# Attention and gated MLP on one core: early silu steps from exponential and reciprocal, one scale of maxima per pair, constants made on the chip, and a new order

## The chip, the cores and the metric

One core of one Trainium2 chip runs the whole program. The time is that of one execution on the device in microseconds; of several executions the median is given. The profile is a hardware trace of one execution. Its engines are PE (matrix multiply, with its weight loads as PEld), DVE (vector), ACT (scalar and activation), POOL (GpSimd) and SP, whose queue issues every DMA of this kernel.

## The reference

Two stages. An attention over 4 batches and 8 heads, 768 positions, head size 64: each query sees the keys less than 16 positions away and, besides, 24 pooled keys (the maximum over each block of 32 keys) with pooled values (the mean over the block).

```python
k_sum = k.reshape(B, H, nb, block, D).max(axis=3)
v_sum = v.reshape(B, H, nb, block, D).mean(axis=3)
scores_l = scale * (q @ k.T)            # kept where |i - j| < 16
scores_s = scale * (q @ k_sum.T) + np.log(block)
a = softmax(concatenate([masked scores_l, scores_s]))
out = a @ concatenate([v, v_sum])
```

Then a gated MLP over the 3072 tokens, d_model 512, d_ff 1536:

```python
g = x @ w_gate
silu = g * (1.0 / (1.0 + np.exp(-g)))
y = (silu * (x @ w_val)) @ w_out
```

The MLP weights arrive as 64-bit floats and are turned into 32-bit floats on the chip.

## The kernel before, in words

**Tiling.** Two heads make a pair `u` (0 to 3), a batch is cut into two halves of 384 tokens, and `k` counts the halves of all batches (0 to 7). A unit `(k,u)` of attention is: scores `SC` on PE (L575), row maxima on DVE, exponentials on ACT, sums and a reciprocal, the scaling `nrm`, two transposes `PP` on PE with copies `pt` back (L701), and the product with the values `XO` (L724). For batch 0 (`k` 0 and 1) the mask and the log of the block size are added on PE, by a matmul of an identity `id_r` with the table `parts_sb` (L602 to L615); the softmax there takes `max0` and `max1` (one per head of the pair, L650), scales each with its own small step `scl0`, `scl1` (L656, L673), and then issues three exponentials per head straight from the score bank (L663). For later batches a fused step does the mask and the minimum (L625).

**Weights.** `w_first(j)` (L961) loads 1 MB of a 64-bit weight tile, for each of the 12 slices `j` of d_ff, and decodes it: `abs` on ACT, then `clamp`, `shift`, `sign` and `low` on DVE (L920), then a split into a high part (ACT) and a low part `lo` (DVE or POOL, L954). `o_first(j)` does the same for the output weights. Later batches use sums of the weight blocks (`weight_sums`, L984); for the first two slices the sums are put off: the tile is written to DRAM as `whole` and read back as `m_again` (`deferred_sums`, L979).

**MLP, batch 0.** `u_plain(j,hf)` (L1043) makes the two products g and v for slice `j` and half `hf`. In `finish` (L1073) ACT takes the silu of g out of the bank into `a`, DVE multiplies `a` by v (`mul`), and `hidden` (L1028) splits it into `hh` and `hl`, which the output matmuls `downs` (L1203) read. Batches 1 to 3 use seven products instead of eight (`u_seven`, L1112).

**Constants.** The table of masks and logs `raw_parts`, the identity `id_sb`, and `mean_sb`, the matrix that pools the values of batch 0 in `first_means` (L762), come by DMA from arrays that the host fills; `parts_sb` and `id_r` are casts of the first two. A score bias `bias_sb` for the later batches is loaded too.

**What sets the order.** Every step is entered in a plan with the engines that may do it and a cost for each. `order` (L295) and `run` (L330) place the steps in a modelled time line: each step gets a latest start, an engine takes the ready step that is due first, and a step that two engines can do goes to the one on which it would end first, after `BIAS` has been added (POOL 0.3, the others 0). `NUDGES` (L219) then moves the due time of named steps, pins some to an engine (`d`, `a`, `p`), and gives PE steps a slack. The result is the fixed order of instructions on each engine and of the DMAs on SP's queue. Where the model sees PE idle early on, small matmuls on zeros (`warm_up`, L1215) are put in front of the next PE step; N_WARM of them open the program.

**Activation tables.** Exponential and silu need different tables on ACT; the profile shows an ACT_TABLE_LOAD ahead of the first step of the other kind.

Of the kernel before, what the change touches and what calls it, by code (L numbers as in the profile page):

```python
# [13 lines left out]
AF = mybir.ActivationFunctionType  # L14
# [7 lines left out]
P = 128  # L22
# [15 lines left out]
GROUP = 3  # L38
DEFER = 2
AGAIN = 5  # L40
# [22 lines left out]
def bias_parts() -> np.ndarray:  # L63

    m = np.zeros((P, 3 * KC + 2 * NB), np.float32)
    first = m[:, : 3 * KC].reshape(P, 3, KC)
    first[:] = score_bias()
    x = np.float32(math.log(BLK) / SCALE)
    for to in (first[:, :, KW:], m[:, 3 * KC : 3 * KC + NB], m[:, 3 * KC + NB :]):
        part = (x.view(np.uint32) & np.uint32(0xFFFF0000)).view(np.float32)  # L70
        to[:] = part
        x = np.float32(x - part)
    return m


def value_pool() -> np.ndarray:

    m = np.zeros((P, NV, NB), np.float32)
    for i in range(WIN, WIN + S):
        m[i % P, i // P, (i - WIN) // BLK] = 1.0 / BLK  # L80
    return m
# [138 lines left out]
kt(0,1) -217.9; q(0,1) -205.2; raw_parts -367.5; id_sb -346.1; mean_sb -133.9; vn(1) -330; vr(1) -256.6  # L220
kt(0,3) -191.9; q(0,3) -127.9; kt(0,0) -97; q(0,0) -125.6; kt(0,2) -102.3; q(0,2) -159.2; bias_sb +527.7
scl0(0,1) -121.6 d; eps(0,1) -37.9 d; scl0(0,3) +606.1 d; max1(0,3) -78.6; scl1(0,3) +52.2 d; nrm(0,3) -176.1 d
fv(2) +158.7 a; scl0(0,0) +51.6 d; eps(0,0) +82.2 a; rcp(0,0) -492.6; nrm(0,0) -235.8 p; pt0(0,1) +183.4 d
pt1(0,1) -91.3 d; FV(0) s0.8; max1(0,2) -216.4; exp5(0,2) +22.8; pt1(0,3) -207.7 a; odd1(1) -6.3 d; odd2(1) -66.4 p
# [12 lines left out]
raw_o4 +49.6; abs_o4 +203.3; shift_o4 -135.6; sign_o4 -36.5; mul(4,0) +271.7; hl(0,4,0) -227.1 p; kw(2,0) +190.1
vt(1,0) +188.9; pool(1,0) +471.8; vpool(1,0) +177.6; join(2,1) +148.4 p; ttr1(2,0) +650.5; exp1(2,0) -158.7
exp2(2,0) -36.6; exp3(2,0) +112.8; nrm(2,0) -156.9 p; ttr1(2,1) +373.4; exp1(2,1) -153.2; exp2(2,1) -95.1
eps(2,1) -86.9 a; silu(4,1) -38.3; clamp_w5 +467.6; low_w5 +74.3; lo_w5 -92.2 d; sumA11_w5 +165 p  # L240
sumA12_w5 +485.6 p; silu(5,0) +131.1; hl(0,5,0) +49.9 p; PP0(2,0) s2.8; pt0(2,0) -351 d; pt1(2,0) +1.5 d
pt0(2,1) +57.2; pt1(2,1) +160.5 a; mul(5,1) +224.1; hh(0,5,1) -381.6 d; hl(0,5,1) +59.7; again_w0 -34.5
sumA21_w0 -60.8 p; part(0,1,0) +157.3; q(2,2) +242.5; join(2,3) +96.7 p; XO(2,0) s0; vw(2,2) +246; vw(2,3) +479.5
exp1(2,2) +286.6; eps(2,2) -309.4 p; rcp(2,2) +73.9; ttr0(2,3) -224.2; ttr1(2,3) -122.4; exp1(2,3) +123.8
eps(2,3) +423 a; rcp(2,3) -179.7; abs_w6 +264.2; low_w6 -37; sumA21_w6 +120.4 p; raw_o6 +291.7; lo_o6 +410.1
hl(0,6,0) +119.7 d; PP0(2,2) s0.3; vs(1,2) +53.8; pt1(2,2) -139.4; vs(1,3) +41.4; hh(0,6,1) -103.9 a
hl(0,6,1) +199.7 p; sumA12_w1 +145 d; sf1 +377.4; sign_w7 -82.7; low_w7 -588.1; sumA22_w7 +111.2 d; sumA11_w7 +188 d
hl(0,7,0) +189.5; kw(3,1) +382.5; join(3,1) +22 d; XO(2,2) s3.7; exp3(3,0) +164.5; nrm(3,0) +341.8; exp3(3,1) +184
eps(3,1) +300; hh(0,7,1) +77.4 a; hl(0,7,1) -202.1 p; clamp_w8 +88.4; sumA22_w8 -305.2 p; sumA11_w8 +68.3 d
sumA12_w8 +178.9; raw_o8 +167.1; clamp_o8 -237.8; shift_o8 +118.5; hi_o8 +250.6; lo_o8 +571.8 d; silu(8,0) +242.2  # L250
hl(0,8,0) +240 p; hl(0,8,1) -72.5 d; pt0(3,0) -78.2 d; pt0(3,1) -83.9 d; q(3,2) +318.7; join(3,2) +22.3 p
kw(3,3) +51.2; XO(3,0) s4.1; nrm(3,2) +412.4 d; shift_w9 -231.9; lo_w9 -70.4 p; sumA12_w9 -232.8 p; mul(9,0) +212.2
hl(0,9,0) -138.2 p; values(3,2) -76.3 p; clamp_w10 +82.9; shift_w10 -137.4; low_w10 +319; sumA21_w10 +300.1
sumA11_w10 -50.7 p; raw_o10 +169.9; abs_o10 +355.1; clamp_o10 -369.2; shift_o10 +77.9; sign_o10 +171.1
clamp_w11 +194.6; hl(0,11,1) -195.9 p; B21l(1,0) +249.6; B22l(1,0) +236.2 p; T3h(1,1) +143.4 d; B21h(1,1) +211.6 d
B22l(1,1) +158.2 p; sh(0) +72 a; hl(1,0,0) +153.4; kw(4,0) -304.1; vpool(2,0) +153; kw(4,1) -142.5; pool(2,1) +156.5
# [176 lines left out]
def body(ctx, tc, qP, kP, kW, vT, vW, vN, vR, wgv, wo, bias, parts, ident, mean, out):  # L433
# [89 lines left out]
    def load_const(b, src, n):  # L523
        add_dma(b.name, n, lambda: make(b), lambda: src, (), (b,))
# [965 lines left out]
```

## Time and profile before

| | |
|---|---|
| median of 3 runs | 678.46 us (678.29 to 680.05) |
| the profiled execution | 681.53 us |
| its span, first to last instruction | 679.8 us |
| PE busy | 667.9 us (98%) |
| DVE busy | 513.2 us (76%) |
| ACT busy | 340.8 us (50%) |
| POOL busy | 124.4 us (18%) |
| mean granted PE clock | 0.995 of full speed |

A row of a timeline gives start, duration, engine, line, operation, tiles written and read, the number of instructions merged, and in brackets the idle time before with what ended it. Rows of groups give the count, the total busy time, the mean duration in ns, and the idle time before. PE's busy time includes the matmuls on zeros and matmuls that run slowly, so a busy PE is not the same as a PE that gets on with its work.

### The profile page before, as it was taken

To read this page: it belongs to the slowest core of one execution; us is meant where nothing else is said; L and a number is where in the kernel's file an instruction comes from. 1 tells how busy PE (TensorE), PEld (TensorE's weight loads), DVE (VectorE), ACT (ScalarE), POOL (GpSimd) and SP (SyncE) were. 2 spreads that over 40 slices of the span, in tenths; PEclk is the share of its full clock that TensorE was granted. 3 is DMA by queue.
4 is the path that set the end of the run, shared out by engine and by line. 5 is a ranking of instruction groups with operands and counts; after the bars stand their busy time and mean duration, and the time that the engine had idled before them with its cause. 6 is when DMAs were issued, how large, how long until landed. Compare 5 with 4: busy or idle time off the path is not lost.

```text
span 679.8 us, 13325 instructions
## 1 busy us (share of the span) xinstructions
PE 667.9 (98%) x5097; PEld 616.2 (91%) x5097; DVE 513.2 (76%) x1135; ACT 340.8 (50%) x850; POOL 124.4 (18%) x115
## 2 busy tenths in 40 slices
PE   8999999999999999999999999999999999999997
PEld 8789899899899998989999898989999898989896
DVE  4899998999999786977758883766768762646464
ACT  2888757677664386644544265744535233313130
POOL 0615306504412130112413140100001000000000
PEclk8999999999999999999999999999999999999999
DMA  9999558878657588785957584663715462535232
GB/s 326 374 341 351 186 215 305 319 273 286 226 200 256 219 283 289 256 282 198 279 227 232 189 301 144 248 212 136 248 39 204 181 221 104 218 108 217 109 109 93
DMA packets 40111, 153.06 MB, mean 225 GB/s; under 512 B 4400, under 2 KB 9328, under 8 KB 33136
## 3 DMA queue, kind: packets, MB, share of 16 engines
q1 hardware_dynamic: 40048, 152.21, 63.5%
q8 instruction: 40, 0.66, 0.4%
q14 instruction: 23, 0.19, 0.1%
HBM read 116.54 MB, written 35.65 MB: 224 GB/s over the span
## 4 chain that ended last, share of the span: by engine, by line
PE 76%; DVE 11%; DMA 7%; issue 2%; ACT 2%; POOL 1%; SPq 0%; DVEq 0%; ACTq 0%; POOLq 0%
PE p L1105 37%; PE acc L1177 25%; PE g L1064 4%; PE v L1064 3%; PE sc L598 3%; PE xo L747 2%; PE pp L714 2%; DVE m_w L949 1%; DVE m_w L943 1%; DMA s<-ss 1%; DMA kw<-in_kW 1%; DMA s<-sf 1%; DVE w L489 1%; DMA raw_w<-in_wgv 1%; DVE m_w L930 1%
## 5 line engine op out<-in xcount | busy, mean ns | idle before, releaser
L1177 PE MATMUL acc<-o,hh 128*128 128x512 f32 x570 | 177.3, 392 | 0.0
L1177 PEld LDWEIGHTS acc<-o,hh 128*128 128x128 f32 x570 | 105.7, 188 | 21.9 <-issue 1.0
L1105 PE MATMUL p<-xh_T,s 128*128 128x384 f32 x432 | 122.6, 339 | 0.9 <-DVE s L489 0.4
L1177 PE MATMUL acc<-o,hl 128*128 128x512 f32 x285 | 111.4, 391 | 0.0
L1105 PE MATMUL p<-xh_B,wa 128*128 128x384 f32 x288 | 84.8, 335 | 0.0
L1105 PEld LDWEIGHTS p<-xh_T,s 128*128 128x128 f32 x432 | 79.0, 188 | 3.1 <-DMA s<-ss 1.1
L484 ACT COPY s<-p 128x384 f32<-128x384 f32 x61 | 29.2, 479 | 90.5 <-PE p L1105 83.3
L1105 PE MATMUL p<-xl_T,s 128*128 128x384 f32 x216 | 72.3, 335 | 0.0
L489 DVE TENSOR_TENSOR part<-acc,part 128x512 f32<-128x512 f32 x71 | 47.5, 685 | 29.0 <-PE acc L1177 29.0
L1177 PEld LDWEIGHTS acc<-o,hl 128*128 128x128 f32 x285 | 53.5, 188 | 11.6 <-DVE hl L489 0.3
L641 ACT ACTIVATE p<-p,nm 128x120 f32<-128x120 f32 x144 | 55.2, 385 | 11.7 <-DVE nm L629 10.2
L489 DVE TENSOR_TENSOR c<-p,u 128x384 f32<-128x384 f32 x72 | 39.6, 552 | 20.2 <-PE p L1105 20.2
L1064 PE MATMUL g<-xh_B,w 128*128 128x384 f32 x192 | 54.1, 340 | 0.4 <-DVE w L489 0.3
L1064 PE MATMUL v<-xh_B,w 128*128 128x384 f32 x192 | 53.2, 335 | 0.0
L1105 PEld LDWEIGHTS p<-xh_B,wa 128*128 128x128 f32 x288 | 53.0, 188 | 0.1
L484 ACT CAST hh<-a 128x384 fp32r<-128x384 f32 x47 | 24.1, 514 | 51.5 <-DVE a L489 47.6
L489 DVE TENSOR_TENSOR hl<-a,hh 128x384 fp32r<-128x384 f32 x77 | 45.9, 596 | 3.6 <-ACT hh L484 0.4
L1105 PE MATMUL p<-xl_B,wa 128*128 128x384 f32 x144 | 48.1, 334 | 0.0
L489 DVE TENSOR_TENSOR a<-c,a 128x384 f32<-128x384 f32 x65 | 40.7, 626 | 5.1 <-ACT a L1040 2.5
L1105 PE MATMUL p<-xh_B,s 128*128 128x384 f32 x144 | 42.4, 334 | 0.0
L1105 PE MATMUL p<-xh_T,wa 128*128 128x384 f32 x144 | 42.3, 334 | 0.0
L1105 PEld LDWEIGHTS p<-xl_T,s 128*128 128x128 f32 x216 | 40.6, 188 | 0.3
(151 smaller groups left out, 1353.8 us busy)
## 6 DMA issues: line engine op xcount, KB each, us to landing
wa<-wa SPq DMA_DIRECT2D x36, 768.0 KB, 4.3
s<-ss SPq DMA_DIRECT2D x24, 1024.0 KB, 7.2
raw_w<-in_wgv SPq DMA_DIRECT2D x12, 1024.0 KB, 6.6
ss<-s SPq DMA_DIRECT2D x12, 1024.0 KB, 7.6
wa<-w SPq DMA_DIRECT2D x12, 768.0 KB, 5.5
kw<-in_kW SPq DMA_DIRECT2D x24, 360.0 KB, 5.6
vw<-in_vW SPq DMA_DIRECT2D x28, 288.0 KB, 4.9
kt<-in_kP SPq DMA_DIRECT2D x16, 400.0 KB, 5.5
```

The costliest lines, as they stand in the source:

```text
L484: nc.scalar.copy(out, in_)
L489: vector[e].tensor_tensor(out=out, in0=a, in1=b, op=op)
L598: nc.tensor.matmul(make(sc[h])[s * QT : (s + 1) * QT, c * KC + at : c * KC + at + x.shape[-1]], make(q)[hs, qs], x, start=not biased or c ...
L641: nc.scalar.activation(out=make(p)[:, i, :], in_=make(p)[:, i, :], func=AF.Exp, scale=-1.0, bias=make(nm)[:, i : i + 1], accum_out=make(sm ...
L714: nc.tensor.transpose(make(pp)[:KC, c * P : (c + 1) * P], make(p)[:, g * NT // 2 + c, :], make(id_sb))
L747: nc.tensor.matmul(ps[hs, qs], v, make(pt)[:, h, qs], start=True, stop=True)
L930: lambda e: nc.vector.tensor_scalar(out=make(m), in0=make(m), scalar1=F64_LO, scalar2=F64_HI, op0=ALU.max, op1=ALU.min), (), (m,),
L943: lambda e: nc.vector.scalar_tensor_tensor(out=bits(), in0=high(), scalar=-0x40000000, in1=bits(), op0=ALU.bitwise_and, op1=ALU.bitwise_or ...
L949: lambda e: nc.vector.scalar_tensor_tensor(out=bits(), in0=low(), scalar=29, in1=bits(), op0=ALU.logical_shift_right, op1=ALU.bitwise_or), ...
L1064: nc.tensor.matmul(t[:, :TOK], a, x, start=u == order_of[0] and i == 0, stop=u == order_of[-1] and i == 2,)
L1105: nc.tensor.matmul(t[:, :TOK], a, x, start=first and kk == 0 and n == 0, stop=kk == 1 and n == 2, skip_group_check=not first,)
L1177: nc.tensor.matmul(ps[:, :wide], a, w, start=j == js[0] and m == 0, stop=j == js[-1] and m == 2)
```

## The change

Seven things are changed.

1. **Silu from the exponential.** For the first half (`hf == 0`) of slices 0 to 3, silu is made as g / (1 + exp(-g)): ACT takes exp(-g) out of the bank into `a`; `more` adds one (DVE or ACT); `inv` takes the reciprocal on DVE; `gate` multiplies by g from the bank on DVE. `mul` and the rest follow as before.
2. **One scale.** `scl` scales the six maxima of a pair in one step after both maxima.
3. **Constants on the chip.** `raw_parts`, `id_sb` and `mean_sb` are filled by memsets (DVE or POOL) and by affine selects on POOL; three DMAs and three input arrays go.
4. **Put-off sums.** AGAIN goes from 5 to 10, so `deferred_sums` for slices 0 and 1 stand after slices 10 and 11.
5. **Reserve behind DMAs.** In the model a DMA that ends between 60 and 215 us counts as 2.5 us later for steps of DVE, ACT and POOL.
6. **Bias.** BIAS of DVE goes from 0 to 0.5, and `join` may also be put on ACT.
7. **Nudges.** The whole table NUDGES is replaced by another, so the order on each engine and of the DMAs comes out anew.

```diff
+BY_EXP = 4
+ONE_SCALE = True
-AGAIN = 5
+AGAIN = 10
...
+SAFE, SAFE_FROM, SAFE_TO = 2.5, 60.0, 215.0
-BIAS = {DVE: 0.0, ACT: 0.0, POOL: 0.3}
+BIAS = {DVE: 0.5, ACT: 0.0, POOL: 0.3}
...
+vn(1) -212.9; kt(0,3) +7.8; q(0,3) +11.6; kt(0,0) +11.9; q(0,0) +9; kt(0,2) +8.9; q(0,2) +11.6; vn(0) +11.4
...
+        more = SAFE if s.engine == DMA and SAFE_FROM < s.end < SAFE_TO else 0.0
-            at[o] = max(at[o], (s.end + lag) if o.after[s] else s.start)
+            at[o] = max(at[o], s.end + lag + more * (not {PE, DMA} & set(o.engines)) if o.after[s] else s.start)
...
+    def make_constants():
+        masks = lambda: make(raw_parts)[:, : 3 * KC].rearrange("p (v c) -> p v c", c=KC)
+        add_fill("id one", id_sb, None, P, lambda: make(id_sb), 1.0)
+        add_choose("id here", id_sb, None, P, lambda: make(id_sb), [[-1, P]], 0, ALU.is_equal, 0.0)
+        logs = log_parts()
...
+            add_fill(f"log{x}", raw_parts, f"l{x}", NB, to, logs[x])
+        add_fill("mask none", raw_parts, "m", 3 * KW, lambda: masks()[:, :, :KW], 0.0)
+        for s in range(2):
...
+            add_choose(f"mask{s} above", raw_parts, "m", 3 * KW, to, [[0, 3], [-1, KW]], 2 * WIN - 1, ALU.is_ge, MASK)
+            add_choose(f"mask{s} below", raw_parts, "m", 3 * KW, to, [[0, 3], [1, KW]], -1, ALU.is_ge, MASK, rows=-1)
+        add_fill("mask first", raw_parts, "m", WIN, lambda: masks()[:QT, 0, :WIN], MASK)
+        add_fill("mask last", raw_parts, "m", WIN, lambda: masks()[QT:, 2, WIN + QT : KW], MASK)
+        add_fill("mean all", mean_sb, None, NV * NB, lambda: make(mean_sb), 1.0 / BLK)
+        add_choose("mean above", mean_sb, None, NV * NB, lambda: make(mean_sb), [[P, NV], [-BLK, NB]], -WIN, ALU.is_ge, 0.0)
+        add_choose("mean below", mean_sb, None, NV * NB, lambda: make(mean_sb), [[-P, NV], [BLK, NB]], WIN + BLK - 1, ALU.is_ge, 0.0, rows=-1)
...
-            f"join({k},{u})", (POOL, DVE), NT * NB, lambda: make(kw)[:, :, KW:],
+            f"join({k},{u})", (POOL, DVE, ACT), NT * NB, lambda: make(kw)[:, :, KW:],
...
-                plan.add(f"scl{g}({k},{u})", {DVE: 0.14, ACT: 0.18}, lambda e, g=g: shrink(e, g), (), ((nm, g),))
...
+                elif g == 1:
+                    plan.add(f"scl({k},{u})", {DVE: 0.14, ACT: 0.18}, lambda e: shrink(e, None), (), (nm,))
...
+    def silu_by_exp(name, a, src, reads):
+        plan.add(
+            f"{name}", {ACT: 0.49},
+            lambda e: nc.scalar.activation(out=make(a), in_=src(), func=AF.Exp, scale=-1.0), reads, (a,), table="exp",
+        )
...
+        plan.add(f"more{name[4:]}", {DVE: cost(DVE, "scalar", TOK), ACT: cost(ACT, "copy", TOK)}, one_more, (), (a,))
+        plan.add(f"inv{name[4:]}", {DVE: 0.53}, lambda e: nc.vector.reciprocal(out=make(a), in_=make(a)), (), (a,), port=False)
+        add_tt(f"gate{name[4:]}", (DVE,), TOK, lambda: make(a), src, lambda: make(a), ALU.mult, reads, (a,))
...
-            silu(f"silu({j},{hf})", a, lambda: make(ps["g"])[:, :TOK], (ps["g"],))
+            by = silu_by_exp if hf == 0 and j < BY_EXP else silu
+            by(f"silu({j},{hf})", a, lambda: make(ps["g"])[:, :TOK], (ps["g"],))
```

More of the change, by code (lines that the diff above doesn't have):

```diff
@@ L60, in score_bias, with log_parts @@
     return m
[L63 to L67, printed above, removed]
+def log_parts() -> list:
+    out = []
     x = np.float32(math.log(BLK) / SCALE)
-    for to in (first[:, :, KW:], m[:, 3 * KC : 3 * KC + NB], m[:, 3 * KC + NB :]):
+    for _ in range(3):
         part = (x.view(np.uint32) & np.uint32(0xFFFF0000)).view(np.float32)
-        to[:] = part
+        out.append(float(part))
         x = np.float32(x - part)
[L73 to L81, printed above, removed]
+    return out
 PE, DVE, ACT, POOL, DMA = "PE", "d", "a", "p", "q"
@@ L219 @@
 NUDGES = """
[L220 to L224, printed above, removed]
@@ L240 @@
[L240 to L244, printed above, removed]
@@ new lines @@
+part(0,1,5) +78; abs_w6 +29.7; sumA12_w6 -6.1 d; wa6 +113.8; hl(0,6,0) +26.2 p; PP1(2,3) s2.3; hh(0,6,1) -38.8 d
+abs_w7 -169.2; sign_w7 +84.5; low_w7 +84.5; hi_w7 -51; sumA21_w7 +52 p; hl(0,7,0) -8.3 d; q(3,0) +133.3
+join(3,0) +51.4 a; join(3,1) +43.9 a; XO(2,3) s1.3; exp0(3,1) +65.6; rcp(3,1) +112.4; nrm(3,1) +12.1 d
+clamp_w8 +91.8; lo_w8 -91.5 p; sumA12_w8 +1.4 d; sf8 +59.7; clamp_o8 +224.2; shift_o8 +37.1; sign_o8 -25.3
+lo_o8 +109.8 d; silu(8,0) +124.7; hl(0,8,0) -79.4 p; hh(0,8,1) -36.3 d; PP0(3,0) s7.9; pt0(3,0) -83.2 d
@@ L432, in body @@
 @with_exitstack
-def body(ctx, tc, qP, kP, kW, vT, vW, vN, vR, wgv, wo, bias, parts, ident, mean, out):
+def body(ctx, tc, qP, kP, kW, vT, vW, vN, vR, wgv, wo, bias, out):
     nc = tc.nc
@@ L521, in body, with add_fill, add_choose @@
     mean_sb = buf("pro", "mean", [P, NV, NB], "mean_sb")
+    def add_fill(name, b, part, cols, to, value):
+        plan.add(
+            name, {DVE: 0.1 + 0.0006 * cols, POOL: 0.1 + 0.0012 * cols},
+            lambda e: vector[e].memset(to(), value), (), ((b, part),),
+        )
+    def add_choose(name, b, part, cols, to, pattern, base, keep, other, rows=1):
+        plan.add(
+            name, {POOL: 0.1 + 0.0012 * cols},
+            lambda e: nc.gpsimd.affine_select(
+                out=to(), in_=to(), pattern=pattern, compare_op=keep, fill=other, base=base, channel_multiplier=rows,
+            ), (), ((b, part),),
+        )
+    def make_constants():
[3 more added lines that the diff above has]
+        logs = log_parts()
+        for x, to in enumerate((lambda: masks()[:, :, KW:], lambda: make(raw_parts)[:, 3 * KC : 3 * KC + NB], lambda: make(raw_parts)[:, 3 * KC + NB :])):
+            add_fill(f"log{x}", raw_parts, f"l{x}", NB, to, logs[x])
+        add_fill("mask none", raw_parts, "m", 3 * KW, lambda: masks()[:, :, :KW], 0.0)
+        for s in range(2):
+            rows = slice(s * QT, (s + 1) * QT)
+            to = lambda rows=rows: masks()[rows, :, :KW]
+            add_choose(f"mask{s} above", raw_parts, "m", 3 * KW, to, [[0, 3], [-1, KW]], 2 * WIN - 1, ALU.is_ge, MASK)
[5 more added lines that the diff above has]
+        add_choose("mean below", mean_sb, None, NV * NB, lambda: make(mean_sb), [[-P, NV], [BLK, NB]], WIN + BLK - 1, ALU.is_ge, 0.0, rows=-1)
     def load_const(b, src, n):
@@ L672, in a_softmax @@
                 plan.add(f"max{g}({k},{u})", {DVE: 0.50}, lambda e, g=g: greatest(g), (sc[g],), ((nm, g),))
-                plan.add(f"scl{g}({k},{u})", {DVE: 0.14, ACT: 0.18}, lambda e, g=g: shrink(e, g), (), ((nm, g),))
+                if not ONE_SCALE:
+                    plan.add(f"scl{g}({k},{u})", {DVE: 0.14, ACT: 0.18}, lambda e, g=g: shrink(e, g), (), ((nm, g),))
+                elif g == 1:
+                    plan.add(f"scl({k},{u})", {DVE: 0.14, ACT: 0.18}, lambda e: shrink(e, None), (), (nm,))
             else:
@@ L1036, in hidden, with one_more @@
         )
+    def silu_by_exp(name, a, src, reads):
+        plan.add(
+            f"{name}", {ACT: 0.49},
+            lambda e: nc.scalar.activation(out=make(a), in_=src(), func=AF.Exp, scale=-1.0), reads, (a,), table="exp",
+        )
+        def one_more(e):
+            if e == ACT:
+                nc.scalar.activation(out=make(a), in_=make(a), func=AF.Copy, bias=1.0)
+            else:
+                vector[e].tensor_scalar(out=make(a), in0=make(a), scalar1=1.0, scalar2=None, op0=ALU.add)
+        plan.add(f"more{name[4:]}", {DVE: cost(DVE, "scalar", TOK), ACT: cost(ACT, "copy", TOK)}, one_more, (), (a,))
+        plan.add(f"inv{name[4:]}", {DVE: 0.53}, lambda e: nc.vector.reciprocal(out=make(a), in_=make(a)), (), (a,), port=False)
+        add_tt(f"gate{name[4:]}", (DVE,), TOK, lambda: make(a), src, lambda: make(a), ALU.mult, reads, (a,))
     def silu(name, a, src, reads):
@@ L1313, in body @@
         if u == 1:
[L1314 to L1315 removed]
+            make_constants()
             add_copy("parts", (POOL, ACT, DVE), 3 * KC + 2 * NB, lambda: make(parts_sb), lambda: make(raw_parts), (raw_parts,), (parts_sb,))
             add_copy("idr", (POOL, ACT, DVE), P, lambda: make(id_r), lambda: make(id_sb), (id_sb,), (id_r,))
[L1318 removed]
             load_first_values(1)
```

88 lines of the change are left out of this document (36 added, 52 removed).

## The prediction

> **What bounds the kernel now.** I read the busy time by stage first, then PE's groups and what they wait for, then the timelines of the first 60 us.
>
> ```profile
> core 0: us, PE busy (x) PEld busy (x) DVE busy (x) ACT busy (x) POOL busy (x), PEclk, DMA share, GB/s
> 10.00:20.00 10.00, 10.00 (x172) 8.55 (x163) 6.37 (x15) 3.77 (x21) 0.99 (x2) 0.66 1.03 411
> 20.00:60.00 40.00, 37.36 (x524) 34.19 (x524) 39.69 (x62) 34.48 (x96) 18.24 (x18) 1.00 0.96 358
> 60.00:220.00 160.00, 158.33 (x1275) 144.94 (x1273) 153.22 (x326) 107.27 (x249) 53.98 (x44) 1.00 0.73 255
> 220.00:670.00 450.00, 449.08 (x3037) 416.55 (x3036) 309.71 (x726) 193.45 (x485) 51.04 (x49) 1.00 0.57 199
> ```
> ```profile
> L1218 PE MATMUL pp<-warm 128*128 128x128 f32 x22 | 3.0, 284 | 0.7 <-DVE xl_B L489 0.7
> ...
> L1218 PE MATMUL xo<-warm 128*128 128x128 f32 x16 | 2.2, 281 | 0.7 <-ACT p L665 0.7
> ```
>
> From 220 us on PE is busy 449.08 of 450 us: it sets the pace there, and no edit takes a matmul of the MLP away. From 60 to 220 us only 1.67 us are free. From 20 to 60 us PE is idle for 40 - 37.36 = 2.64 us, and 3.0 + 2.2 = 5.2 us of its busy time are matmuls on zeros, put where the plan expected PE to wait: 7.8 us in which PE gets nowhere. DVE is busy 39.69 of these 40 us, ACT 34.48, POOL only 18.24. So this stage belongs to DVE, with ACT close behind. The other open time is the start, before the first scores. I sum the edits against the profiled execution, 681.53 us; the median of the runs, 678.46, lies 3.07 us below it.
>
> **Constants on the chip.** SP's queue at the start, the landing of the query that PE waits for, how full the DMA engines are, and the sizes:
>
> ```profile
> 0.72 0.39 SPq L503 DMA_DIRECT2D raw_parts<-in_parts  x1
> 1.16 0.42 SPq L503 DMA_DIRECT2D id_sb<-in_ident  x1
> ...
> 3.04 0.43 SPq L503 DMA_DIRECT2D q<-in_qP  x1
> ```
> ```profile
> 3.04 5.80 DMA q<-in_qP
> ```
> ```profile
> 6.00:8.00 2.00, 1.64 (x15) 1.45 (x14) 0.54 (x1) 0.51 (x1) 0.00 (x0) 1.00 1.03 382
> ```
> ```profile
> raw_parts<-in_parts SPq DMA_DIRECT2D x1, 204.0 KB, 2.5
> ...
> id_sb<-in_ident SPq DMA_DIRECT2D x1, 64.0 KB, 2.2
> ```
>
> The query lands at 8.84 us, with the DMA engines full (1.03). Ahead of it go 268 KB that fall away: at 382 GB/s 0.7 us. By issues it is more: the new nudges put `vn(1)` first and leave key and query to their own due times, so the query could be third, at 0.72 + 2 x 0.44 = 1.6 us, 1.4 us earlier. I take 0.9 us, nearer to the bytes, as the engines are full. The third load, `mean_sb`, stands behind the query.
>
> What takes the place of the DMAs is POOL work: one identity select, four mask selects of 288 columns and two of 168, besides fills that DVE can share. No select is in this trace. The nearest rows are a copy with one input and a step with two:
>
> ```profile
> L486 POOL COPY kw<-ks 128x144 f32<-128x144 f32 x11 | 6.2, 568 | 40.4 <-PE p L1105 24.4 <-DMA kw<-in_kW 8.9 <-issue 4.1
> ```
> ```profile
> L489 POOL TENSOR_TENSOR m_w<-m_w 128x256 f32<-128x256 f32 x18 | 21.4, 1197 | 35.5 <-ACT w L484 24.2 <-DVE w L489 7.7 <-DVE m_w L489 2.6
> ```
>
> The five selects for identity and mask take 2.9 us at 0.57 each, 6.0 us at 1.2 each, from about 0.8 us on. The table is wanted when the first scores run, near 8.0 us after the edit, with two casts ahead of it. I take no cost: at the dearer row POOL ends near 7 us. If a select costs 2 us, the first scores come some 3 us late. Term: -0.9.
>
> **One scale.**
>
> ```profile
> L661 DVE TENSOR_SCALAR nm<-nm 128x3 f32<-128x3 f32 x8 | 1.6, 214 | 0.0
> ```
>
> Sixteen small scales, eight of them on DVE as this row shows, become eight: about 0.8 us of DVE, half of it in the stage that it binds, so -0.4 in DVE's sum below. The added wait: the exponentials of the first head wait for the second maximum as well, and behind them on ACT wait the rest of that unit and the copies `pt`. Where both maxima stand side by side on DVE this is nothing; elsewhere it is what DVE puts between them, and the plan can give ACT other work. I take 0, up to 0.5 us.
>
> **Silu from the exponential.** What ACT does around the first silu, PE beside it, and the loads that bring the exponential back:
>
> ```profile
> 45.47 1.28 ACT L1040 ACT_TABLE_LOAD   x1
> 46.77 0.49 ACT L1040 ACTIVATE a<-g 128x384 f32<-128x384 f32 x1
> 47.15 0.20 ACT L659 ACTIVATE nm<-nm 128x3 f32<-128x3 f32 x1
> 47.37 1.28 ACT L665 ACT_TABLE_LOAD   x1
> ...
> 50.36 0.88 ACT L484 COPY pt<-pp 120x384 f32<-120x384 f32 x2
> ```
> ```profile
> 48.92 0.87 PE L714 MATMUL pp<-id_sb,p 128*120 128x128 f32 x6
> 50.54 1.60 PE L1218 MATMUL xo<-warm 128*128 128x128 f32 x12 [0.75 <-ACT p L665]
> ```
> ```profile
> L665 ACT ACT_TABLE_LOAD x3 | 3.8, 1283 | 0.1
> ```
>
> Three loads bring the exponential back, and each has one to silu before it: six loads, 7.7 us of ACT, of which all but one to silu fall away. The first two, 2.57 us, stand ahead of the copies `pt` at 50.36. PE's transposes end at 49.79 and the product starts at 52.1: 2.3 us lost. Without the loads the two copies can follow the transposes at once, 0.9 us, and PE loses 0.9 to 1.0: I take -1.4 (0 if DVE delivers the scores later, -1.7 if DVE takes one copy). The loads after 60 us meet a PE with 1.67 us to win: -0.5. The Trainium skill, ScalarE: Activation LUTs, section What ACT_TABLE_LOAD costs, adds about 1.38 us of drain to each load; here the next ACTIVATE starts 0.02 us after the load ends (45.47 + 1.28, then 46.77), so the trace disagrees; by the page the six loads would be worth 16 us of ACT, an estimate, not 7.7.
>
> DVE pays for it. The rows for `more`, `gate` and `inv`, and last the copies and casts that DVE does from 20 to 60 us (its column is the first):
>
> ```profile
> L486 DVE CAST hh<-a 128x384 fp32r<-128x384 f32 x49 | 18.6, 379 | 0.9
> ...
> L489 DVE TENSOR_TENSOR a<-v,a 128x384 f32<-128x384 f32 x24 | 13.1, 547 | 0.0
> ```
> ```profile
> L690 DVE RECIPROCAL ri<-sm x32: 147/180/192, 19.2 to 495.1; 128x6 f32<-128x6 f32 x32
> L687 DVE TENSOR_SCALAR sm<-sm x8: 160/170/174, 19.0 to 461.8; 128x6 f32<-128x6 f32 x8
> ```
> ```profile
> 20.00:60.00 40.00, 2.53 (x6) 8.71 (x11) 1.00 0.96 358
> ```
>
> `more` is 0.38, `gate` 0.55. For `inv` the trace has reciprocals of 6 columns only. Beside the scalar step of the same 6 columns their median is 10 ns longer and their shortest 13 ns shorter, so the nearest row shows no price per column. Low end: 0.55, as `gate`. Middle: the 10 ns as a price of 6 columns, 64 x 10 ns = 0.64 more, 1.2 us. (A far higher end is the last rival.) I take 0.55. A step is then 1.48 us, and three of the four fall before 60 us: +4.4. Against it stand the scales, -0.4, and the copies: with 0.5 of bias against DVE and an ACT that is 7.7 us lighter, most of the 2.53 us can go to ACT: -2.2. POOL has 21.8 us free there, and I expect one low part or one scaling of a unit to pass to it: -1.5. DVE's sum: +0.3, from -1 (more passes) to +3 (`inv` at 1.2, less passes).
>
> **Reserve, put-off sums, bias of `join`.**
>
> ```profile
> DVE kw L486 <- DMA kw<-in_kW: 7.8, 6, 2.2
> ```
> ```profile
> 200.00:220.00 20.00, 20.00 (x146) 18.59 (x145) 19.83 (x41) 10.55 (x21) 3.96 (x2) 1.00 0.69 240
> ```
> ```profile
> L489 POOL TENSOR_TENSOR m_again<-m_again 128x256 f32<-128x256 f32 x4 | 4.2, 1055 | 6.2 <-DMA m_again<-whole 3.1 <-DVE m_again L489 2.9
> ```
>
> DVE stands 7.8 us behind late loads of `kw`, with all its later steps queued behind that `join`. A reserve, or `join` on ACT, puts other work first. But PE has 1.67 us to win, 0.5 of it counted: -0.7, from 0 to -1.2. Moving the sums takes their two loads and two stores on SP, and four POOL steps of 1.06 us, away from slices 5 and 6 and adds them near 200 us, where POOL is busy 3.96 of 20 us but DVE 19.83. I cost that at nothing because POOL covers it; if DVE gets them, the late one is the first store of sums, which the seven products need from about 226 us: 1 to 2 us. After 220 us PE has 0.92 us free, so a new order wins next to nothing there and can lose: 0, up to +2.
>
> **The sum.** -0.9 - 1.4 - 0.5 + 0.3 - 0.7 = -3.2: 678.3 us as a profiled execution, 675.3 beside the median. All terms at their best: -1.4 - 1.7 - 0.5 - 1.0 - 1.2 = -5.8, 672.7. At their worst: -0.7 + 3 + 2 = +4.3, 682.8. About 0.3% (2 us) is what a measurement of this kernel can tell from no change.
>
> **The rivals.**
>
> *The clock stays up (more gain).*
>
> ```profile
> 13.00:18.00 5.00, 5.00 (x48) 3.92 (x40) 2.77 (x6) 1.36 (x8) 0.00 (x0) 0.50 1.03 415
> ```
>
> From 13 to 18 us PE is granted half its clock, and nobody else is full (DVE 2.77, ACT 1.36 of 5 us). If earlier first scores escape that, these 5 us of matmuls shrink toward 2.5; I count 2 of it: 673.3. For it: the query comes earlier. Against: the same small matmuls follow in the same order of units.
>
> *Nothing is won (the same).* DVE's stage does not move: what ACT is spared waits behind DVE anyway, and three steps of 1.48 us eat what copies and scales give. Then the start remains, less up to 1 us: 677.6 to 678.5.
>
> *The reciprocal is long (slower).* From the copies of DVE a fixed part can be read: 379 ns for 384 columns above and
>
> ```profile
> L486 DVE COPY kw<-ks 128x144 f32<-128x144 f32 x13 | 2.9, 225 | 7.8 <-DMA kw<-in_kW 7.8
> ```
>
> give 0.64 ns a column and 133 ns fixed. If the reciprocal has that fixed part, its 180 ns leave 47 ns for 6 columns, 7.8 ns each, and 384 of them take 3.1 us. Three such steps hold DVE 3 x 2.55 = 7.7 us longer where it is full; less the 3.2 us that the rest gives, +4.5: 683. It decides against the change from `inv` = 0.55 + 3.2/3 = 1.6 us. Against it: the scalar step of 6 columns, nearer in shape, has no smaller a time. The Trainium skill, VectorE: DVE Perf Modes, section First, the fixed hardware budget, calls the reciprocal an iterative divide with a repeat count of 8, which speaks for this rival; the trace has no wide one and leaves it open.
>
> **How the numbers follow.** Forecast 0.46, clock stays up 0.13, nothing won 0.20, long reciprocal 0.16, late mask or late sums 0.05 (about 681). Faster 0.59, same 0.20, slower 0.21. The forecast's own range is 672.7 to 677; the whole one runs from 669.5, the clock's rival with the best terms, to 681.5, and leaves out most of the long reciprocal.
>
> **What would show it.** Right: no table load between the first exponentials and the first true silu, scores from about 8 us, fewer zeros ahead of `xo` near 50 us, `inv` at 0.55 us, DVE full from 20 to 60 us. Wrong: `inv` over 1.6 us, selects on POOL past 8 us, or PE waiting after 220 us.

## The result and the profile after

The kernel with the change takes 689.27 us (median of 4 runs, 686.51 to 690.79), the kernel before in the same comparison 678.38 us (678.22 to 680.05): a ratio of 1.015, 95% interval 1.0114 to 1.0187. It is slower by 10.9 us, where 3.2 us less was forecast. The profiled execution took 688.82 us with a span of 687.1 us. PE is busy 668.0 us in it, against 667.9 before, so of the 7.3 us by which this span is longer all but 0.1 are idle time of PE. (The profiled execution of before lies 3.07 us above its median, so the medians stand further apart than the spans.) Where that time lies, stage by stage, after:

```profile
core 0: us, PE busy (x) PEld busy (x) DVE busy (x) ACT busy (x) POOL busy (x), PEclk, DMA share, GB/s
20.00:60.00 40.00, 34.95 (x485) 32.11 (x481) 39.84 (x56) 29.99 (x84) 13.86 (x13) 0.96 1.00 369
60.00:90.00 30.00, 25.78 (x239) 21.92 (x238) 27.79 (x40) 17.12 (x47) 6.42 (x5) 1.00 0.46 151
90.00:220.00 130.00, 130.00 (x1028) 120.61 (x1027) 124.47 (x254) 88.51 (x207) 51.22 (x49) 1.00 0.77 271
220.00:440.00 220.00, 219.57 (x1574) 202.05 (x1572) 155.77 (x362) 127.34 (x308) 65.26 (x54) 1.00 0.67 235
440.00:470.00 30.00, 27.34 (x259) 23.55 (x254) 18.55 (x72) 18.54 (x62) 1.38 (x5) 0.94 0.62 206
```

And the two later stages of before:

```profile
60.00:90.00 30.00, 29.06 (x264) 26.45 (x262) 28.05 (x44) 21.15 (x50) 10.86 (x8) 1.00 0.72 250
440.00:470.00 30.00, 30.00 (x239) 27.27 (x238) 19.90 (x60) 14.24 (x42) 0.00 (x0) 1.00 0.47 163
```

PE loses 37.36 - 34.95 = 2.4 us from 20 to 60 us, 3.3 us from 60 to 90, and 2.7 us from 440 to 470, a stretch for which the prediction had only "0, up to +2". DVE is still full from 20 to 60 us (39.84 of 40), while ACT fell from 34.48 to 29.99 and POOL from 18.24 to 13.86: what ACT was spared did not become time of PE. The wide reciprocal, which no trace of before held, beside the narrow one:

```profile
L1067 DVE RECIPROCAL a<-a 128x384 f32<-128x384 f32 x4 | 10.2, 2546 | 0.0
L706 DVE RECIPROCAL ri<-sm 128x6 f32<-128x6 f32 x32 | 5.6, 180 | 10.3 <-POOL sm L703 5.9 <-ACT sm L701 4.0
```

One `inv` takes 2.55 us, not 0.55, and 378 more columns cost 2546 - 180 = 2366 ns, 6.26 ns each. PE's largest waits:

```profile
PE acc L1210 <- DVE a L469: 3.3, 2, 2.4
PE acc L1210 <- ACT hh L464: 2.7, 1, 2.7
PE pp L730 <- DVE p L709: 2.6, 2, 2.2
```

The first and third lie in the stages with reciprocals, the second is the one near 450 us. In the timeline of PE the two that come out of the early stages are these, the idle time in brackets:

```profile
48.18 1.51 PE L730 MATMUL pp<-id_sb,p 128*120 128x128 f32 x6 [2.17 <-DVE p L709]
...
66.00 0.73 PE L1210 MATMUL acc<-o,hh 128*128 128x512 f32 x2 [2.44 <-DVE a L469]
```

How the reciprocal gets there is seen on DVE ahead of the first one. After:

```profile
42.26 2.55 DVE L1067 RECIPROCAL a<-a 128x384 f32<-128x384 f32 x1
44.72 0.47 DVE L664 TENSOR_REDUCE nm<-sc 128x3 f32<-128x360 f32 x1
45.10 0.54 DVE L469 TENSOR_TENSOR a<-g,a 128x384 f32<-128x384 f32 x1
45.56 0.52 DVE L664 TENSOR_REDUCE nm<-sc 128x3 f32<-128x360 f32 x1
46.00 0.18 DVE L706 RECIPROCAL ri<-sm 128x6 f32<-128x6 f32 x1
46.10 0.52 DVE L469 TENSOR_TENSOR a<-v,a 128x384 f32<-128x384 f32 x1
...
47.13 0.90 DVE L709 TENSOR_TENSOR p<-p,ri 128x720 f32<-128x720 f32 x1
```

There is no bracket: DVE never stops. `nrm` (L709) stands in the queue behind `inv` though it needs nothing from it, and ends at 48.03; the transposes on PE wait for it and start at 48.18. A gap of PE can also cost what follows it. The clock granted to PE (the third column from the end) in the two stretches after this gap, after the one of 2.44 us that ends at 66 us, and after the one near 450 us that is told next:

```profile
48.00:50.00 2.00, 1.82 (x8) 1.85 (x9) 2.00 (x3) 1.74 (x7) 0.60 (x1) 0.50 1.00 412
50.00:52.00 2.00, 2.00 (x10) 2.00 (x9) 2.00 (x4) 1.28 (x4) 0.00 (x0) 0.65 1.01 413
...
66.00:68.00 2.00, 2.00 (x20) 1.46 (x22) 2.00 (x4) 0.51 (x1) 0.61 (x1) 1.00 0.00 0
...
454.00:456.00 2.00, 2.00 (x8) 1.43 (x8) 1.52 (x3) 0.23 (x1) 0.00 (x0) 0.54 0.05 20
```

After two of the three gaps the clock fell, after the one at 66 us it did not.

The loss near 450 us has another cause. POOL, then DVE behind it, then PE:

```profile
446.68 0.30 POOL L466 COPY kw<-ks 128x144 f32<-128x144 f32 x1 [7.34 <-PE p L1138]
447.07 0.23 POOL L703 TENSOR_SCALAR sm<-sm 128x6 f32<-128x6 f32 x1
450.96 0.30 POOL L466 COPY kw<-ks 128x144 f32<-128x144 f32 x1 [3.66 <-DMA kw<-in_kW]
451.35 0.23 POOL L703 TENSOR_SCALAR sm<-sm 128x6 f32<-128x6 f32 x1
```
```profile
451.62 0.19 DVE L706 RECIPROCAL ri<-sm 128x6 f32<-128x6 f32 x1 [2.95 <-POOL sm L703]
```
```profile
453.81 0.93 PE L1210 MATMUL acc<-o,hh 128*128 128x512 f32 x2 [2.66 <-ACT hh L464]
```

These are `join(7,0)`, the small step `eps(6,2)` on the sums of unit (6,2), `join(7,1)` and `eps(6,3)`. `join(7,1)` waits 3.66 us for a late load of `kw`, and `eps(6,3)`, which needs no load, stands behind it on POOL. DVE waits 2.95 us for that step, the casts `hh` on ACT come late, and PE waits 2.66 us. So two suspects come out of the trace: the price of `inv`, and the place of one `join`.

### The profile page after: what moved, and what is told of

Same layout as the page of the kernel before. It is cut to its first block, busy times and chain, and to the rows that moved or that the text cites. A ratio compares the mean times of both kernels' runs of the same rounds, so it can differ in the third digit from the quotient of the medians.

```text
span 687.1 us, 13339 instructions
## 1 busy us (share of the span) xinstructions
PE 668.0 (97%) x5083; PEld 614.8 (89%) x5083; DVE 501.9 (73%) x1043; ACT 366.6 (53%) x912; POOL 160.6 (23%) x164
## 4 chain that ended last, share of the span: by engine, by line
PE 80%; DVE 9%; DMA 7%; ACT 1%; issue 1%; POOL 1%; SPq 0%; DVEq 0%; ACTq 0%; POOLq 0%
PE p L1138 34%; PE acc L1210 27%; PE g L1096 6%; PE v L1096 6%; PE xo L763 3%; PE sc L611 2%; PE pp L730 2%; DMA s<-ss 2%; DVE a L1067 1%; DMA raw_w<-in_wgv 1%; DMA kw<-in_kW 1%; DMA s<-sf 1%; DMA whole<-m_w 1%; DMA q<-in_qP 1%; DVE p L709 1%
## 5 line engine op out<-in xcount | busy, mean ns | idle before, releaser
L464 ACT CAST hh<-a 128x384 fp32r<-128x384 f32 x78 | 40.0, 513 | 77.6 <-DVE a L469 76.8
L464 ACT COPY s<-p 128x384 f32<-128x384 f32 x65 | 31.2, 479 | 69.2 <-PE p L1138 68.7
L469 DVE TENSOR_TENSOR hl<-a,hh 128x384 fp32r<-128x384 f32 x75 | 44.9, 599 | 16.6 <-ACT hh L464 13.8
L469 DVE TENSOR_TENSOR a<-c,a 128x384 f32<-128x384 f32 x62 | 38.9, 628 | 6.1 <-ACT a L1072 3.7
L469 DVE TENSOR_TENSOR u<-p,s 128x384 f32<-128x384 f32 x36 | 19.9, 553 | 32.1 <-ACT s L464 30.6
```

What stands on the lines that cost most here:

```text
L464: nc.scalar.copy(out, in_)
L469: vector[e].tensor_tensor(out=out, in0=a, in1=b, op=op)
```

## The experiments

Each ran in turn with the kernel before on one chip, in three batches (experiments 1, 2, 3 and 5; then 7; then 4, 6 and 8), the third on another chip than the first two; the median of the kernel before was 679.86, 679.01 and 678.92 us. So batches are compared by their ratios to it, and a gain in us is a ratio times 679 us. Unless it is said otherwise, the order of the steps on each engine is that of the kernel named, so that nothing but the edit differs.

**1. The reciprocal made short (theory: price of `inv`; rival: the new order itself is bad).** In the kernel after, `inv` keeps its place but is a multiplication. Here, in 3 and for half of the steps in 4, the kernel leaves out the reciprocal, so its values are not those of silu:

```diff
-        plan.add(f"inv{name[4:]}", {DVE: 0.53}, lambda e: nc.vector.reciprocal(out=make(a), in_=make(a)), (), (a,), port=False)
+        plan.add(f"inv{name[4:]}", {DVE: 0.53}, lambda e: tt(e, make(a), make(a), make(a), ALU.mult), (), (a,), port=False)
```

> The changed kernel with every instruction in its place, only that `inv` multiplies `a` by itself instead of taking the reciprocal, so the gate's value is not silu. Theory 1, the wide reciprocal (2.55 us in the trace, four of them) starves PE between 40 and 85 us: `inv` falls to about 0.55 us, DVE is relieved of 8 us, PE's waits on DVE at 48, 66 and 73 us shrink, and the time falls by 4 to 6 us, to 683 to 685. Rival, the new order and not the reciprocal is what costs: the waits move to the next late step of DVE and the time stays at 687 or above. The wait near 451 us stays in either case.

Measured: 680.0 us, ratio 1.0011 (0.9989 to 1.0032). Against the 1.015 of the kernel after that is 0.0139, about 9.4 us, for four steps that are 4 x 2.0 = 8.0 us shorter on DVE. The price of the reciprocal is thus most of the loss. That the loss is more than the length of the steps is not shown: the intervals of the two ratios leave about 3 us either way.

**2. The join moved (theory: the late load blocks POOL; rival: the loss near 450 us follows from the early one).** In the kernel after, one step changes its place on POOL:

```diff
-    for s in order(plan.steps):
+    line = order(plan.steps)
+    late = next(s for s in line if s.name == "join(7,1)")
+    line.remove(late)
+    line.insert(1 + next(i for i, s in enumerate(line) if s.name == "eps(6,3)"), late)
+    for s in line:
```

> The changed kernel with one step moved: on POOL, join(7,1) goes behind eps(6,3) instead of ahead of it. Theory 2, one small POOL step stood behind a join that waits for a late load, and through it DVE, ACT and PE stood still near 451 us: the wait of PE on `hh` (2.7 us) and the half clock after it go, and the time falls by 4 to 4.5 us, to about 685. Rival, something else is late there as soon as this is gone (the scaling, the table load): less than 2 us. Rival 2, the stall is there in only some executions, since the spread of the changed kernel is 4 us: the fastest runs stay at 686.5 and only the slow ones come down.

Measured: 686.76 us, ratio 1.0103 (1.0075 to 1.0130): 0.0047 less, about 3.2 us. The stage, of the kernel with the join moved:

```profile
440.00:470.00 30.00, 30.00 (x318) 26.57 (x317) 21.20 (x77) 21.79 (x71) 3.38 (x8) 1.00 0.70 230
```

PE is busy throughout; from 20 to 90 us it is not, with 34.53 of 40 and 25.76 of 30 us, as in the kernel after. In experiment 1 the stall near 450 us was still there (27.82 of 30 us). So each loss is there without the other. The intervals of 1.015 and 1.0103 overlap, and the fastest runs of the two kernels, 686.51 and 686.35 us, are alike, which the second rival (a stall in some executions only) would give as well. Against it stands the same move made on the kernel of experiment 1, in one batch (experiment 3): the median falls from 680.0 to 677.4 us and the fastest run from 678.33 to 675.68. The move is worth 2.6 to 3.7 us.

**3. Both.** Edits 1 and 2 together.

> Both edits: the short `inv` (not silu's value) and join(7,1) behind eps(6,3). If the two causes are independent, the gains add, 8 to 10.5 us, and the time is 679 to 681, within 3 us of the kernel before. If the order as such costs something more, it stays above 682.

Measured: 677.4 us, ratio 0.9956 (0.9933 to 0.9979). The gains add up: 0.0139 + 0.0047 = 0.0186 against the 0.0194 from 1.015 to 0.9956. With both causes taken away no loss is left. DVE of this run, to set beside the timeline of the kernel after:

```profile
41.98 0.55 DVE L469 TENSOR_TENSOR a<-a 128x384 f32<-128x384 f32 x1
42.45 0.53 DVE L664 TENSOR_REDUCE nm<-sc 128x3 f32<-128x360 f32 x1
42.89 0.55 DVE L469 TENSOR_TENSOR a<-g,a 128x384 f32<-128x384 f32 x1
43.35 0.52 DVE L664 TENSOR_REDUCE nm<-sc 128x3 f32<-128x360 f32 x1
43.79 0.18 DVE L706 RECIPROCAL ri<-sm 128x6 f32<-128x6 f32 x1
43.89 0.52 DVE L469 TENSOR_TENSOR a<-v,a 128x384 f32<-128x384 f32 x1
...
45.23 0.90 DVE L709 TENSOR_TENSOR p<-p,ri 128x720 f32<-128x720 f32 x1
```

The same steps in the same order; from the start of `inv` to that of `nrm` it is 3.25 us instead of 4.87.

**4. Two reciprocals of four (does each cost the same, or only those before 60 us?).** As 3, but slices 0 and 1 keep the true reciprocal.

```diff
+            lambda e: nc.vector.reciprocal(out=make(a), in_=make(a)) if name in ("silu(0,0)", "silu(1,0)") else tt(e, make(a), make(a), make(a), ALU.mult),
```

> The changed kernel with join(7,1) behind eps(6,3); `inv` is the true reciprocal for slices 0 and 1 and a multiplication (not silu's value) for slices 2 and 3. None true gave 677.4, four true 686.8. If each reciprocal costs PE its 2 us of DVE wherever it stands: half way, 681.5 to 682.5. If, as the prediction had it, only those ahead of 60 us count (slices 0, 1 and the third's start): 683 to 685. If the late ones count because PE had run out of stock by then: 678.5 to 680.5.

Measured: 680.67 us, ratio 1.0028 (1.0014 to 1.0042). From 0.9956 with none to 1.0103 with four, two give 0.0072 of 0.0147, half: within the intervals the two after 60 us cost as much as the two before. The stages agree. From 20 to 60 us PE is busy 34.73 us, as with all four (34.53; 36.97 with none), and from 60 to 90 us 29.04, as with none (25.76 with all four).

**5. A silu without the reciprocal.** As 3, but silu as 0.5 g (1 + tanh(g/2)): ACT takes the tanh in place of the exponential, `more` and `inv` issue nothing, `gate` does (a + 1) g, and `mul` brings the factor 0.5. It is the same function in another form.

```diff
-            lambda e: nc.scalar.activation(out=make(a), in_=src(), func=AF.Exp, scale=-1.0), reads, (a,), table="exp",
+            lambda e: nc.scalar.activation(out=make(a), in_=src(), func=AF.Tanh, scale=0.5), reads, (a,), table="exp",
...
-        add_tt(f"gate{name[4:]}", (DVE,), TOK, lambda: make(a), src, lambda: make(a), ALU.mult, reads, (a,))
+            lambda e: nc.vector.scalar_tensor_tensor(out=make(a), in0=make(a), scalar=1.0, in1=src(), op0=ALU.add, op1=ALU.mult),
```

> The whole computation again, in the order of the changed kernel with join(7,1) behind eps(6,3): silu of the early steps as 0.5 g (1 + tanh(g/2)). ACT takes tanh in place of the exponential, `more` and `inv` emit nothing, `gate` is (a + 1) g and `mul` is 0.5 a v, so a step costs DVE 0.55 us beside `mul` instead of 3.5. If the reciprocal was the cost and the edit's idea (one table early) is sound, 1 us or more better than with both edits above: 677 to 680, and no table load between the early exponentials and the first true silu. If avoiding the loads is worth nothing, no better than that kernel.

Measured: 675.87 us, ratio 0.994 (0.992 to 0.9961), below both kernels. Its two early stages:

```profile
20.00:60.00 40.00, 36.97 (x499) 34.03 (x498) 39.34 (x59) 31.66 (x94) 17.16 (x14) 1.00 1.01 376
60.00:90.00 30.00, 29.86 (x260) 26.30 (x259) 27.77 (x42) 20.50 (x42) 5.49 (x4) 1.00 0.72 250
```

The loss of 60 to 90 us is gone (25.78 there in the kernel after).

**6. What the saved table loads are worth in the new order.** As 5, but silu comes from its own table: the six early loads are back and DVE has none of the added steps.

```diff
+            lambda e: nc.scalar.activation(out=make(a), in_=src(), func=AF.Silu), reads, (a,), table="exp",
...
+        plan.add(f"gate{name[4:]}", on((DVE,), "tt", TOK), lambda e: None, reads, (a,))
```

> The order of the changed kernel with join(7,1) behind eps(6,3), every step in its place, but the early silu steps are the true silu of ACT's table again (`more`, `inv` and `gate` emit nothing): the table loads come back and DVE has nothing to pay. Against the same kernel with tanh (675.9 us, ratio 0.994) this gives the price of the loads alone in this order. If the loads are worth what the prediction said (1.4 + 0.5 us, less DVE's `gate` of 3 x 0.55): within 1.5 us, 675.5 to 677.5. If ACT is the late engine in this order: 679 to 682. If what ACT is spared waits behind DVE anyway, as in the old order: 674 to 676.

Measured: 679.64 us, ratio 1.0011 (0.9992 to 1.003), so 0.0071 or 4.8 us slower than 5, though DVE has four steps less. The stage and a pair of loads in it, in this run:

```profile
20.00:60.00 40.00, 35.30 (x488) 32.57 (x487) 36.29 (x52) 35.70 (x93) 15.11 (x13) 1.00 1.02 381
```
```profile
39.98 1.28 ACT L1057 ACT_TABLE_LOAD   x1
41.28 0.49 ACT L1057 ACTIVATE a<-g 128x384 f32<-128x384 f32 x1
41.77 1.28 ACT L678 ACT_TABLE_LOAD   x1
```

Behind the second load come the exponentials of a unit, and DVE waits for their sums:

```profile
45.51 0.19 DVE L706 RECIPROCAL ri<-sm 128x6 f32<-128x6 f32 x1 [2.93 <-ACT sm L701]
```

DVE has 3.7 us idle in the stage, 2.93 of them here, and PE is still short. In this order dropping the loads is worth about two and a half times the 1.9 us that the prediction gave them, once nothing long takes their place.

**7. Parts of the change in the kernel before.** Its order is kept throughout. The constants alone (memsets and selects as in the change, at the places of the three DMAs):

> The kernel before, its order kept, with one part of the change alone: masks, identity and pooling matrix filled on POOL and DVE instead of loaded. Predicted in the sum: 0.9 us earlier first scores (0.7 to 1.4). In the trace of the changed kernel the first scores start at 7.91 instead of 8.97 us. Expected 677 to 677.8 if that gain lasts to the end; 678.4 if DVE's backlog after 20 us eats it; 675 to 676.5 if the earlier start also keeps PE's clock from halving at 11 to 18 us.

Measured: 677.09 us, ratio 0.9967 (0.9953 to 0.9982), a gain of 2.2 us. But the first scores start hardly earlier than in the kernel before (8.97 us there):

```profile
8.78 0.35 PE L640 MATMUL sc<-kt,q 64*64 64x96 f32 x2 [1.05 <-DMA q<-in_qP]
```

Part of the gain is the clock between 10 and 20 us. The profiled run of the kernel before had the dip to half clock there and a mean granted clock of 0.995 over the whole run; this one had no dip, and a mean of 0.999. Of the 25 runs of the kernel before in this batch, 9 show a mean of 0.993 to 0.995, with a median of 680.46 us, and the other 16 one of 0.998 or more, with 678.36 us. All ten runs with the constants show 0.999 or more. Beside the runs of before without the dip, 677.09 us is a gain of 1.3 us.

The early silu alone, its four steps together where `silu` stood:

```diff
+            nc.scalar.activation(out=make(a), in_=src(), func=AF.Exp, scale=-1.0)
+            nc.vector.tensor_scalar(out=make(a), in0=make(a), scalar1=1.0, scalar2=None, op0=ALU.add)
+            nc.vector.reciprocal(out=make(a), in_=make(a))
+            tt(DVE, make(a), src(), make(a), ALU.mult)
```

> The kernel before, its order kept, with the early silu steps from the exponential alone (hf 0, slices 0 to 3; add, reciprocal and gate on DVE right behind the exponential). Theory 1: DVE gets 4 x 3.4 us more where it is full, of which ACT's six saved table loads give back 1 to 2 us: 6 to 11 us slower, 685 to 689. Rival, the reciprocal's time hides beside other work: within 2 us of before.

Measured: 693.88 us, ratio 1.0203 (1.0171 to 1.0234): 13.8 us slower by the ratio, more than expected. PE's waits in it:

```profile
PE xo L747 <- DVE pt L486: 4.3, 1, 4.3
PE pp L714 <- POOL p L693: 3.4, 1, 3.4
```

The early silu alone, by tanh (no reciprocal, and the six loads saved):

> The kernel before, its order kept, with the early silu steps as 0.5 g (1 + tanh(g/2)): no reciprocal, one step of 0.55 us on DVE more per early silu, six table loads fewer. If the loads are worth what the prediction gave them (1.4 + 0.5 us) less 3 x 0.55 of DVE: 677.5 to 678.5. If ACT's relief is worth more in a place where it is not seen, 675 to 677; if DVE's order is what binds alone, 679 to 680.

Measured: 680.64 us, ratio 1.0024 (1.0008 to 1.0039): 1.6 us slower. The loads are gone, DVE has four `gate` steps of 0.55 us more, and nothing is gained. ACT and PE near 50 us in this run, where the prediction looked for 1.4 us:

```profile
47.45 0.36 ACT L665 ACTIVATE p<-sc,nm 128x120 f32<-128x120 f32 x1 [1.84 <-DVE nm L661]
```
```profile
48.98 1.60 PE L1231 MATMUL xo<-warm 128*128 128x128 f32 x12 [0.72 <-ACT p L665]
```

ACT, which in the kernel before spent that time on loads, now waits 1.84 us for DVE's scale, and PE's wait of 0.75 us is still there as 0.72. With the old order this is the rival "nothing is won": what ACT is spared waits behind DVE.

Constants and tanh together:

> The kernel before, its order kept, with the constants made on the chip and the early silu steps from tanh. If the two are independent, the sum of the two kernels above: 676 to 677.5, faster than the kernel before and the changed one. If both only shorten the wait for the same late DVE step, no better than the better of the two.

Measured: 678.59 us, ratio 0.9996 (0.9978 to 1.0015). The sum of the parts would be 0.9967 + 0.0024 = 0.9991, within the interval; a gain is not shown, and the 676 to 677.5 us that were expected were missed.

**8. The order made anew.** The kernel after with the true price in the plan, `inv` 2.47 instead of 0.53:

> The changed kernel whole, but the plan is told that `inv` takes 2.47 us instead of 0.53, so the order is made anew with the true length (the join near 451 us falls where the plan puts it). Theory 1, DVE is full and 8 us more cannot be hidden by any order: PE's progress by 100 us as poor as in the changed kernel, 685 to 690. Rival, the length was harmless and only its wrong price in the plan put other steps behind it: 3 us or more better in the first 100 us, 680 to 684.

Measured: 710.78 us, ratio 1.0461 (1.0439 to 1.0484). The kernel of experiment 5 without `more` and `inv` in the plan, without the moved join, and with the reserve kept up to 600 us:

> Silu of the early steps from tanh with `more` and `inv` gone from the plan too, so that the order is made anew without them, nothing moved by hand, and the reserve behind DMAs reaching to 600 us instead of 215. If theory 2 holds in general (a reserve keeps small steps of POOL out from behind a late join), no wait of several us after 220 us, and 674 to 677, faster than the kernel before by 0.3% or more. If a new order draws a new stall, 679 or above.

Measured: 697.21 us, ratio 1.0269 (1.0245 to 1.0293). Both are far worse than the kernels whose order they replace, with waits that those do not have; of the first and of the second:

```profile
PE acc L1251 <- DVE a L469: 4.8, 1, 4.8
```
```profile
PE p L1141 <- DVE s L471: 7.4, 4, 2.6
```

In both, NUDGES is the table that the change brought. That its due times, pins and slacks fit only the one plan for which they were set is how I read it; what was measured is that a truer price with the same table costs 21 us. The first run lies far above both of its expectations, and the second is the case of a new stall. Experiment 8 therefore tells nothing about the reserve or about a better order.

## Why the prediction was wrong

The step that failed is the price of `inv`: "Low end: 0.55, as `gate`. ... I take 0.55". It measured 2.55 us. The rival of the long reciprocal set its point of decision at 1.6 us and its price at 2.55 us more a step; the price is 2.0 us more, well past that point, and experiments 1 and 3 show that it decides. I compared the reciprocal of 6 columns with a scalar step of 6 columns, where the fixed part is some 142 of 180 ns. That row could not speak against a price per column, and the difference that could have, copies of 144 and 384 columns, was put in the rival and not in the forecast. The rival's own 683 us falls short as well, since it counted three steps and had no loss after 220 us. It had a chance of 0.16.

Point by point:

- **How many count.** Three steps before 60 us were reckoned. The groups of this stage show two in the kernel after, the other two follow at 62.18 and 70.02 us, and all four count (experiment 4). "From 60 to 220 us only 1.67 us are free" was room to gain; I read it as if nothing there could be lost.
- **The size of the loss.** Four steps of 2.0 us are 8.0 us; experiment 1 gives 9.4 us, which the intervals do not tell apart. The half clock after a gap, seen from 48 to 52 us, would add to it, but was not measured by itself.
- **After 220 us.** "0, up to +2" held no mechanism. The `join` in front of `eps(6,3)` costs about 3 us (experiments 2 and 3). The prediction's own words on late loads of `kw`, "with all its later steps queued behind that `join`", named the mechanism, but for DVE. Of the 7.8 us of its row only 3.2 lie before 220 us and 3.3 after 440 (waits of 1.64 and 1.66 us that end at 459 and 461 us), so the trace of before held the warning for the late stage. In the new order it happened on POOL from 447 us, where the reserve, which ends at 215 us, does not reach.
- **Constants.** -0.9 was forecast, from the bytes that no longer stand ahead of the query. Alone they give -2.2 us, or -1.3 beside runs without the clock's dip (experiment 7), but not by that way: the query is issued 0.87 us earlier (at 2.17 instead of 3.04 us) and the first scores start only 0.19 us earlier. Where the rest of the gain comes from is open. The 7.91 us of the kernel after comes with its new order of loads. The selects are hidden, as argued. Their rows, that of the cast which waits for the masks, and that of the first scores:

```profile
L512 POOL TENSOR_SCALAR_AFFINE_SELECT raw_parts<-raw_parts 64x288 f32<-64x288 f32 x4 | 1.7, 437 | 0.4 <-DVE raw_parts L506 0.2
```
```profile
4.64 0.53 ACT L464 CAST parts_sb<-raw_parts 128x408 fp32r<-128x408 f32 x1 [2.19 <-POOL raw_parts L506]
```
```profile
7.91 0.42 PE L611 MATMUL sc<-kt,q 64*64 64x96 f32 x8
```

  A select took 0.44 us, below both bounds, and the table was cast by 5.2 us, well ahead of the scores at 7.9 us ("from about 8 us" was right).
- **Table loads.** "-1.4" and "-0.5" were right for neither order: no gain, with four short DVE steps in their place, in the old one (experiment 7), and about 4.8 us in the new one (experiment 6). The six early loads did fall away, but the new order has six more later on: both kernels have 38 in all.
- **Help from POOL.** "-1.5" for a step passed to POOL: POOL's busy time from 20 to 60 us fell from 18.24 to 13.86 us, so no help of that kind came in sum.
- **The sum of the rest.** With the two causes taken away the kernel is 3.0 us below before (experiment 3), and -3.2 was forecast. This is luck: single terms missed in both directions, and the runs of before in that batch with a full clock (0.998 or more) have a median of 678.85 us, only 1.45 us above 677.4.
- **The clock's rival.** From 10 to 20 us the kernel after has a full clock where before had 0.66. But of two kernels with the early silu alone, which start as before does, the one by tanh and then the one by exponential show both:

```profile
10.00:20.00 10.00, 9.43 (x190) 8.62 (x185) 8.32 (x21) 5.82 (x34) 3.55 (x6) 1.00 1.02 404
```
```profile
10.00:20.00 10.00, 10.00 (x161) 8.70 (x154) 6.44 (x15) 3.98 (x22) 1.21 (x2) 0.66 1.03 410
```

  The dip comes and goes with the same start, so it can't be credited to the change. Nor do the constants keep it away: in the profiled run of constants and tanh together the clock is 0.66 from 10 to 20 us. The rival's price of 2 us was right. The first product with the values (`xo`) starts at 26.63 us in before and 26.35 in constants with tanh, both with the dip, and at 24.18 in tanh alone and 24.13 in constants alone, both without; in whole runs of before the dip is worth 2.1 us (680.46 against 678.36).
- **The range.** The lower end of 669.5 us does not come out of its terms: the best terms give 672.7 us, and 2 us for the clock 670.7.

**Open.** How the gain of the new order divides among one scale, bias, reserve and put-off sums was not settled: each alone draws a new order, and experiment 8 shows what that does. Together they show no gain: the kernel of experiment 6, which has all of them, the constants and one moved `join`, but silu from its own table, stands at 1.0011, the constants alone at 0.9967. If that difference of 3 us is theirs, they cost it with an order that was set for silu without table loads. What makes a clock dip come in one execution and not in the next is open too. One execution of each kernel is profiled, and the runs of the kernel after spread over 4.3 us.

## What to carry to other kernels

Price an operation per column before trusting a narrow row of it: two operations that agree at 6 columns (180 and 170 ns), where the fixed part is most of the time, can differ by a factor of seven at 384 (the reciprocal 2546 ns, the scalar step `more` on DVE 350), and if the bounds of such a price fall on both sides of the deciding point, the dear one has to weigh as much as the cheap one. What an engine is relieved of is worth only what the next late engine lets through (dropping the same six table loads, for four short steps on DVE, brought nothing in one order and 4.8 us in the other), so look at who is late next before counting them. In a fixed order, look on every queue, the idle one too, for a short step that stands behind one that waits for a DMA.

## What the hardware showed that was not expected

The reciprocal on DVE costs 6.26 ns a column with some 142 ns fixed (180 - 6 x 6.26, a line through two widths), ten times the 0.64 ns a column of a copy. The Trainium skill, VectorE: DVE Perf Modes, section First, the fixed hardware budget, calls it an iterative divide with a repeat count of 8; the slope agrees with it in direction.

An affine select on POOL is cheap: 437 ns for 64 partitions of 288 columns, less than the 568 ns that a copy of 144 columns took in the kernel before.

Some gaps of PE of 2 to 3 us were followed by some microseconds at about half the granted clock, and others were not. In the kernel after it was so behind gaps of 2.17 us (0.50 from 48 to 50 us, 0.65 from 50 to 52) and 2.66 us (0.54 from 454 to 456), but not behind one of 2.44 us (1.00 from 66 to 68). In the kernel of experiment 2 the gap at the same place, 2.42 us, was followed by 0.70 and then 0.50 from 66 to 70 us. The length alone does not decide it.

A dip to half clock early on, with PE busy in it, comes in some executions and not in others of one and the same kernel, at a price of about 2 us here.
